# Two output bursts of eight key chunks per unit instead of three, and four fill products per step in the prologue

## The chip, the cores and the metric

The kernel runs on one core of a Trainium2 chip. The metric is the device time of one execution in microseconds (us), the median of several runs; less is better.

## What is computed

Two independent results stand side by side in the output, both in f32 with 2048 rows.

```python
# left half: attention, 32 query heads of width 32, one key head and one value head
q = (x @ wq).reshape(B, S, H, Dh).transpose(0, 2, 1, 3)
k, v = x @ wk, x @ wv
p = softmax(einsum("bhqd,bkd->bhqk", q, k) * Dh ** -0.5)
a = einsum("bhqk,bkd->bhqd", p, v).transpose(0, 2, 1, 3).reshape(B, S, H * Dh) @ wo
# right half: real part of a 2D DFT given as matrices
y = dft_seq_re @ (x2 @ dft_hid_re.T) - dft_seq_im @ (x2 @ dft_hid_im.T)
```

S is 2048 and D is 1024.

## The kernel before

Every engine's order is written out by hand: each instruction keeps its place in the program (the recording helper is line 79, so nearly all rows of the profile carry L79). TensorE (PE) has two kinds of work that are woven together.

**Fill products.** The query projections, the DFT and the output projection are groups of 12 or 24 matmuls of 128x512 into one PSUM bank (`psb`, two banks). An operand is split into a high and a low part, so that a product is three matmuls (`mh`/`ml` against `rh`/`rl`). `take(n)` issues the next n matmuls, `pos["fill"]` counts them, and `pump()` issues the loads, casts and subtractions that are due a given number of products ahead. Left operands live in a ring of NM slots: the cast of item i may only be issued once item i-NM has been used up. When a group is full, VectorE (DVE) takes it out of PSUM; for the query projections that is a TENSOR_SCALAR and a SCALAR_TENSOR_TENSOR (`q_group`).

**Attention.** A unit is four heads for 512 queries; there are 32 units with 32 steps each (SU), 1024 steps in all. A unit goes through two passes.

- The score pass (`scores`, `row_sums`) finds each query's log-sum. A step is two matmuls into a tile of `pss`, a pool of two PSUM tiles; DVE takes the maximum over it (TENSOR_REDUCE), ScalarE (ACT) then does exp in place and sums (ACTIVATE and its ACTIVATION_READ_ACCUMULATOR). After the last step of a unit `lse_1` to `lse_4` combine the sums with small operations, and one transpose (`nm` with `ident`), which also takes a `pss` tile, brings them into the layout that the next pass needs.
- The key pass (`expo`) makes the probabilities. A step is two matmuls into `pst`, one PSUM tile, and an exp on ACT into a tile of the pool `pp` (NP tiles named `p`). The output burst `pv(u, k)` then multiplies the tiles with `v`: four heads times the chunks between `CUT[k]` and `CUT[k + 1]`, as matmuls of 32 columns, which profile rows count twice (24 matmuls stand as x48). A chunk is two steps. DVE adds the burst's bank into `ov`.

The score pass runs LEAD steps and one whole unit ahead of the key pass. So the program has a prologue of SU + LEAD score steps with fill products between them and no key pass, then 1024 steps with a key pair each, in whose last SU + LEAD there are no scores left. `level(n)` spreads the remaining fill products over the steps; a step with a burst has none. `open_unit` loads a unit's queries (`qst`, three buffers), `inverse` loads the reciprocal sums (`rb`), and a unit's scaled output is made by GpSimd (POOL) in `ends` and stored to DRAM.

Of the kernel before, what the change touches and what calls it, by code (L numbers as in the profile page):

```python
# [8 lines left out]
F32 = mybir.dt.float32  # L9
F32R = mybir.dt.float32r  # L10
# [6 lines left out]
P = 128  # L17
# [4 lines left out]
W = 512  # L22
NG = 8
NQ = 4
NC = 16
# [76 lines left out]
def tile_kernel(ctx: ExitStack, tc, xT, wq, wkv, wo, xbT, wT, cT, out):  # L102
    nc = tc.nc
    te = Ordered(tc, nc.tensor)
    act = Ordered(tc, nc.scalar)
    dve = Ordered(tc, nc.vector)
    gp = Ordered(tc, nc.gpsimd)
# [3 lines left out]
    def pool(stack, name, bufs, **kw):  # L111
        kw.setdefault("reuse_waits", "tile")
        return stack.enter_context(tc.tile_pool(name=name, bufs=bufs, **kw))
# [17 lines left out]
    kst = keep.tile([P, S], F32R, name="kst")  # L131
# [6 lines left out]
    ps_t = pool(ctx, "ps_t", 1, space=PSUM)  # L138
    ps_b = [pool(ctx, f"ps_b{i}", 1, space=PSUM) for i in range(2)]

    NR0, NM0, NY = 3, 3, 6
    NR, NM = 14, 4
    r0p = pool(ctx, "r0p", NR0, side="right")
    m0p = pool(ctx, "m0p", NM0, side="right")
    rp = pool(ctx, "rp", NR)
# [43 lines left out]
    pos = {"fill": 0, "s": 0}  # L189
# [82 lines left out]
    ML = Line(NM0, NM, (52, 36, 27, 21), load_m, comb, hi_m, lo)  # L272
# [42 lines left out]
    def at(p, f):  # L315
        k = len(later)
        while k and later[k - 1][0] > p:
            k -= 1
        later.insert(k, (p, f))
# [33 lines left out]
    def bank(name, open_=False):  # L353

        while held:
            held.pop(0)()
        b = 1 - cur["bank"] if cur["bank"] is not None else int(used[1] < used[0])
        cur["at"] += 1
        used[b] = cur["at"]
        if open_:  # L360
            cur["bank"] = b
        return ps_b[b].tile([P, W], F32, name=name)
# [16 lines left out]
    def take(n):  # L379
        for _ in range(n):  # L380
            if cur["group"] >= len(groups):
                return
            g = groups[cur["group"]]
            j = pos["fill"] - g.at
            if j == 0:
                cur["ps"] = bank("psb", True)
            if j % 3 == 0:
                RL.force(g.right[j // 3])
            if j % 12 == 0:
                ML.force(g.left[j // 12])  # L390
            product(g, cur["ps"], j)
            pos["fill"] += 1
            if j == g.n - 1:
                cur["group"] += 1
                assert all(hasattr(it, "done") for it in g.ys)
                g.post(cur["ps"])
                cur["at"] += 1
                used[cur["bank"]] = cur["at"]
                cur["bank"] = None
                if g.ys:  # L400
                    at(pos["fill"] + 2 * BEHIND + 5, lambda n=len(g.ys): yused.__setitem__(0, yused[0] + n))
            pump()
            run_later()
# [300 lines left out]
    start = [q_group(0, g, sets[0]) for g in range(2)]  # L704
# [10 lines left out]

    qsp = pool(ctx, "qsp", 1)
    rows = []
    NP = 13
    pp = pool(ctx, "pp", NP, side="right")
    sm = pool(ctx, "sm", 2, side="right")  # L720
    onp = pool(ctx, "onp", 1, side="right")

    units = [(b, g) for b in range(NQ) for g in range(NG)]
    SU = 32
    LEAD = 12
    total = SU * len(units)
    qst, nm, lse, pt, ov, rb, pend = ({} for _ in range(7))
    ends = []
# [73 lines left out]
            r = r_d[u][4 * h:4 * h + 4].rearrange("t c -> (t c)")  # L802
            sp.dma_start(rb[u][h * DH:(h + 1) * DH], r.unsqueeze(0).to_broadcast([DH, W]))

    def expo(n):
        u, r = divmod(n, SU)
        c, hp_ = divmod(r, 2)
        pt[u, c, hp_] = pp.tile([P, 2, W], F32, name="p")
        ps = ps_t.tile([P, 2, W], F32, name="pst")
        for a in range(2):  # L810
            te.matmul(ps[:, a], kst[:, c * P:(c + 1) * P], qst[u][:, 2 * hp_ + a], start=True, stop=True)
        act.activation(pt[u, c, hp_], ps, AF.Exp)

    CUT = (0, 6, 11, NC)

    def blocks(d, g, x):
        return d[:, :, g].rearrange("t p c -> p t c"), x.rearrange("p (t c) -> p t c", t=4)

    def pv(u, k):

        aside()
        ps = bank("psb")
        for c in range(CUT[k], CUT[k + 1]):
            for h in range(4):
                te.matmul(ps[h * DH:(h + 1) * DH], v[:, c], pt[u, c, h // 2][:, h % 2], start=c == CUT[k], stop=c == CUT[k + 1] - 1)
        if k == 0:
            ov[u] = onp.tile([P, W], F32, name="ov")
            dve.tensor_copy(ov[u], ps)
        else:
            dve.tensor_add(ov[u], ov[u], ps)  # L830
        cur["at"] += 1
        if k == len(CUT) - 2:
            b, g = units[u]
            if b < 2:
                def scaled():
                    o = onp.tile([P, W], F32, name="oh")
                    gp.tensor_mul(o, ov[u], rb[u])
                    store(*blocks(o_d[b], g, o), ("o", b, g))
                ends.append(scaled)
                return  # L840
            hi_ = onp.tile([P, W], F32, name="oh").bitcast(F32R)
            lo_ = onp.tile([P, W], F32R, name="ol")
            lse["out"] = hi_, lo_

            last = u + 1 == len(units)
            e = dve if last else gp

            def low():
                e.tensor_sub(lo_, ov[u], hi_.bitcast(F32))
                if not last:  # L850
                    store(*blocks(oh_d[b], g, hi_))
                    store(*blocks(ol_d[b], g, lo_), ("o", b, g))

            ends.append(lambda: e.tensor_mul(ov[u], ov[u], rb[u]))
            ends.append(lambda: e.tensor_copy(hi_, ov[u]))
            ends.append(low)

    def score_step(s):

        if s < total:  # L860
            u, r = divmod(s, SU)
            if r == SU - 6 and u + 1 < len(units):
                open_unit(u + 1)
        if SU <= s < SU * (len(units) + 1) and s % SU == TURN:
            row_sums(s - 1)
            lse_3((s - SU) // SU)
        if s < total:
            scores(s)
        row_sums(s - 1)
        u, e = divmod(s - SU, SU)  # L870
        if 0 <= u < len(units):
            for f in LSE.get(e, ()):
                f(u)

    TURN = 3
    LSE = {0: (lse_1,), 1: (lse_1b,), 2: (lse_2,), 5: (lse_4,)}

    zeros = v[:, :, :].rearrange("p a b -> p (a b)")
    for n in (W, 3 * P):
        te.matmul(ps_t.tile([P, 2, W], F32, name="pst")[:, 0, :n], zeros[:, :P], zeros[:, :n], start=True, stop=True)  # L880
    room = [t[:, k] for t in [pp.tile([P, 2, W], F32, name="p") for _ in range(NP)] for k in range(2)]
    room += [r0p.tile([P, W], F32, name="r1", bufs=NR0 - 1) for _ in range(2)] + [onp.tile([P, W], F32, name="rb")]
    room += [m0p.tile([P, 4, P], F32, name="m1", bufs=NM0 - 1).rearrange("p a b -> p (a b)") for _ in range(2)]
    room += [r0p.tile([P, W], F32, name="r0", bufs=NR0)]
    xs = [[room[b * ND + c] for c in range(ND)] for b in range(NQ)]

    def load_x(b):
# [12 lines left out]
    wkv_t = onp.tile([P, W], F32, name="ov")  # L900
    sp.dma_start(wkv_t, wkv.rearrange("p a b -> p (a b)"))
    load_x(1)
    for it in start[1].left:
        ML.force(it)
    pump()
    load_x(2)
    load_x(3)
# [5 lines left out]
    take(48)  # L913
    for s in range(SU + LEAD):
        score_step(s)
        take(7)

    PRO = pos["fill"]
    FILL = end[0]
    LAST = 24  # L920


    QUIET = total - SU - LEAD
    MORE = 1

    def goal(n):
        return PRO + (FILL - PRO - LAST - MORE * (total - QUIET)) * n // total + MORE * max(n - QUIET, 0)


    ENDS = [2 * c for c in CUT]  # L930

    def snap(p):

        for d in (0, 1, -1, 2, -2, 3, -3):
            g = next((g for g in groups if g.at <= p + d < g.at + g.n), None)
            j = p + d - g.at if g else 0
            if j == 0 or 6 <= j <= g.n - 6:
                return p + d
        return p

    def level(n):
        r = n % SU
        if r in ENDS:
            return 0, 0
        more = min(e for e in ENDS if e > r) - r
        left = snap(goal(n + more)) - pos["fill"] - (2 if more > 2 else 0)
        fill = max(round(left / more), 0)
        return fill, min(fill, more, 2)

    for n in range(total):  # L950
        u, r = divmod(n, SU)
        if n == total - 12:
            w1 = wo_set(1)
            add([o_group(NQ - 1, t, e, ws) for e, ws in ((0, w0), (1, w1)) for t in range(4)])
        score_step(n + SU + LEAD)
        if ends:
            ends.pop(0)()
        fill, first = level(n)
        take(first)
        expo(n)  # L960
        if r == 16:
            inverse(u)
        if r in ENDS and n:
            pv((n - 1) // SU, (ENDS.index(r) - 1) % (len(CUT) - 1))
        take(fill - first)


    last = groups[len(groups) - 8:]
    take(last[0].at - pos["fill"] - 12)
    pv(len(units) - 1, len(CUT) - 2)  # L970
    while ends:
        ends.pop(0)()
    hi7, lo7 = lse["out"]
# [27 lines left out]
    for t, g in enumerate(last[4:]):  # L1001
        ps = whole(4 + t)
# [41 lines left out]
```

## Time and profile before

| what | value |
|---|---|
| median of 3 runs | 2695.97 us (2695.78 to 2699.55) |
| the profiled execution's own time | 2700.78 us |
| its span, first to last instruction | 2699.0 us |
| mean granted TensorE clock | 0.999 |
| matmul rows on PE | 13820 |

Durations below come from the one profiled execution. Its own time is 1.78 us more than its span and 4.81 us more than the median. A matmul's row is longer than its distance to the next row, since matmuls are pipelined: the distance between the starts is what a matmul costs.

### The profile page before, as it was taken

Reading aid. Unit: us, or ns where it says so; the run is one execution under the profiler, and the core shown is the slowest. Engines: PE = TensorE matmul, PEld = TensorE weight load, DVE = VectorE, ACT = ScalarE, POOL = GpSimd, SP = SyncE. Lnnn points to the kernel's source line nnn. Section 1 sums busy time; section 2 is a strip of 40 time slices with the busy share of each in tenths; the row PEclk is TensorE's granted clock in tenths of the full one; section 3 lists DMA queues with packets and bytes.
Section 4 is the critical chain, followed back from the end, with each engine's and each line's share of the span. In section 5 each row is a group of like instructions: output and inputs, shape, how many; then the busy total and the mean of one; then the engine's idle time right before and its main releaser. Section 6 shows DMA issues by size and latency. Waiting matters only on the chain. (4 is left out here: it accounts for less than half of the span.)

```text
span 2699.0 us, 40566 instructions
## 1 busy us (share of the span) xinstructions
PE 2689.4 (100%) x13820; PEld 1920.5 (71%) x13820; DVE 1593.1 (59%) x1826; ACT 2130.9 (79%) x3131; POOL 1723.3 (64%) x1711
## 2 busy tenths in 40 slices
PE   9999999999999999999999999999999999999999
PEld 6876767677676766767676676767677676766767
DVE  5766666666676665655565566666555555655411
ACT  3588888888888888888888888878888888888741
POOL 4854425776647558875556675576887887865741
PEclk9999999999999999999999999999999999999999
DMA  8543336887788666654445679874775765644665
GB/s 277 188 142 124 114 102 209 283 281 224 255 267 285 204 220 184 194 182 137 144 155 152 187 244 298 294 238 139 212 222 165 223 198 160 207 143 131 194 209 187
DMA packets 316931, 538.24 MB, mean 199 GB/s; under 512 B 35962, under 2 KB 63354, under 8 KB 316666
## 3 DMA queue, kind: packets, MB, share of 16 engines
q1 hardware_dynamic: 315572, 533.69, 62.5%
q8 instruction: 109, 1.79, 0.3%
q10 hardware_dynamic: 1152, 1.97, 0.2%
q14 instruction: 98, 0.80, 0.1%
HBM read 395.58 MB, written 138.15 MB: 198 GB/s over the span
## 5 line engine op out<-in xcount | busy, mean ns | idle before, releaser
L79 DVE TENSOR_REDUCE nm<-pss 128x1 f32<-128x1024 f32 x1024 | 1252.3, 1223 | 550.8 <-PE pss L79 549.7
L79 ACT ACTIVATE p<-pst 128x1024 f32<-128x1024 f32 x1026 | 1056.0, 1029 | 444.6 <-PE pst L79 435.0
L79 ACT ACTIVATE pss<-pss,nm 128x1024 f32<-128x1024 f32 x1024 | 1112.4, 1086 | 53.7 <-DVE nm L79 53.1
L79 PE MATMUL psb<-rh,mh 128*128 128x512 f32 x1790 | 699.2, 391 | 0.2 <-ACT rh L79 0.2
L79 PE MATMUL psb<-rl,mh 128*128 128x512 f32 x1790 | 698.4, 390 | 0.0
L79 PE MATMUL psb<-rh,ml 128*128 128x512 f32 x1790 | 698.3, 390 | 0.0
L79 PE MATMUL pss<-kst,qst 128*128 128x512 f32 x2048 | 642.8, 395 | 0.2
L79 PE MATMUL pst<-qst,kst 128*128 128x512 f32 x2048 | 635.8, 392 | 0.1
L79 POOL TENSOR_TENSOR ml<-m,mh 128x512 fp32r<-128x512 f32 x366 | 473.2, 1293 | 33.3 <-PE pss L79 26.3
L79 PEld LDWEIGHTS pss<-kst,qst 128*128 128x128 f32 x2048 | 375.6, 188 | 128.9 <-issue 51.1
L79 PE MATMUL psb<-p,v 128*32 128x512 f32 x4096 | 461.0, 596 | 3.1 <-DVE y L79 3.1
L79 PEld LDWEIGHTS pst<-qst,kst 128*128 128x128 f32 x2048 | 377.9, 188 | 92.2 <-ACT p L79 16.3
L79 PEld LDWEIGHTS psb<-rh,mh 128*128 128x128 f32 x1790 | 336.6, 188 | 75.9 <-issue 1.7
L79 PEld LDWEIGHTS psb<-rh,ml 128*128 128x128 f32 x1790 | 336.4, 188 | 72.8 <-issue 1.7
L79 PEld LDWEIGHTS psb<-rl,mh 128*128 128x128 f32 x1790 | 336.5, 188 | 71.8 <-DVE rl L79 0.5
L79 POOL CAST mh<-m 128x512 fp32r<-128x512 f32 x365 | 224.6, 615 | 234.1 <-PE psb L79 199.8
L79 PEld LDWEIGHTS psb<-p,v 128*32 128x32 f32 x4096 | 123.6, 110 | 287.6 <-issue 270.2
L79 POOL TENSOR_TENSOR m<-m,m 128x512 f32<-128x512 f32 x220 | 284.4, 1293 | 42.5 <-DMA m<-o 19.6
L79 POOL TENSOR_TENSOR rl<-r,rh 128x512 fp32r<-128x512 f32 x208 | 269.1, 1294 | 4.0
L79 POOL CAST rh<-r 128x512 fp32r<-128x512 f32 x208 | 128.5, 618 | 203.0 <-PE psb L79 152.2
L79 ACT ACTIVATION_READ_ACCUMULATOR pss<-pss,nm 128x1 f32 x1024 | 211.0, 206 | 0.0
L79 POOL TENSOR_TENSOR r<-r,r 128x512 f32<-128x512 f32 x120 | 155.2, 1293 | 62.0 <-DMA r<-in_wT_dram 44.7
(92 smaller groups left out, 791.9 us busy)
## 6 DMA issues: line engine op xcount, KB each, us to landing
m<-in_cT_dram SPq DMA_DIRECT2D x384, 256.0 KB
r<-s SPq DMA_DIRECT2D x192, 256.0 KB
y<-y SPq DMA_DIRECT2D x128, 256.0 KB
r<-in_wT_dram SPq DMA_DIRECT2D x88, 256.0 KB
m<-in_xbT_dram SPq DMA_DIRECT2D x88, 256.0 KB
y<-u SPq DMA_DIRECT2D x80, 256.0 KB
m<-in_wq_dram SPq DMA_DIRECT2D x64, 256.0 KB
qst<-qh SPq DMA_DIRECT2D x64, 256.0 KB
```

The lines of the kernel that those rows point to most:

```text
L79: return lambda *a, **k: self.tc.keep_in_program_order(f(*a, **k))
```

## The change

Each unit's output is multiplied out in two bursts of eight chunks instead of three of six, five and five. The burst follows the unit's step 15 or 31 directly and takes in the tile of that very step: the step's key matmuls come ahead of the burst and its exp is issued after the burst's first chunk, so 15 tiles of `p` (13 before) are enough. LEAD goes from 12 to 20 and the prologue's steps take four products instead of seven. The ring of left operands has three slots instead of four. A unit's scaled output is made in place in `ov` (and `rb`), not in tiles of its own. Queries are opened ten score steps ahead of their unit's first instead of six, the transpose comes one score step later (TURN), and the last burst of all lies inside the loop.

```diff
-    NR, NM = 14, 4
+    NR, NM = 14, 3
...
-    NP = 13
+    NP = 15
...
-    LEAD = 12
+    LEAD = 20
...
-    def expo(n):
+    def key_scores(n):
         u, r = divmod(n, SU)
         c, hp_ = divmod(r, 2)
-        pt[u, c, hp_] = pp.tile([P, 2, W], F32, name="p")
         ps = ps_t.tile([P, 2, W], F32, name="pst")
         for a in range(2):
             te.matmul(ps[:, a], kst[:, c * P:(c + 1) * P], qst[u][:, 2 * hp_ + a], start=True, stop=True)
+        return ps
+
+    def key_exp(n, ps):
+        u, r = divmod(n, SU)
+        c, hp_ = divmod(r, 2)
+        pt[u, c, hp_] = pp.tile([P, 2, W], F32, name="p")
         act.activation(pt[u, c, hp_], ps, AF.Exp)
 
-    CUT = (0, 6, 11, NC)
+    CUT = (0, NC // 2, NC)
+    LASTS = [2 * c - 1 for c in CUT[1:]]
...
-    def pv(u, k):
+    def pv(u, k, between):
...
                 te.matmul(ps[h * DH:(h + 1) * DH], v[:, c], pt[u, c, h // 2][:, h % 2], start=c == CUT[k], stop=c == CUT[k + 1] - 1)
+            if c == CUT[k]:
+                between()
...
-                    o = onp.tile([P, W], F32, name="oh")
-                    gp.tensor_mul(o, ov[u], rb[u])
+                    gp.tensor_mul(o, o, r)
...
-            if r == SU - 6 and u + 1 < len(units):
+            if r == SU - 10 and u + 1 < len(units):
                 open_unit(u + 1)
...
-    TURN = 3
+    TURN = 4
...
     for s in range(SU + LEAD):
         score_step(s)
-        take(7)
+        take(4)
 
     PRO = pos["fill"]
     FILL = end[0]
-    LAST = 24
+    LAST = 12
...
-        expo(n)
+        ps = key_scores(n)
         if r == 16:
             inverse(u)
-        if r in ENDS and n:
-            pv((n - 1) // SU, (ENDS.index(r) - 1) % (len(CUT) - 1))
+        if r in LASTS:
+            pv(u, LASTS.index(r), lambda: key_exp(n, ps))
+        else:
+            key_exp(n, ps)
         take(fill - first)
...
-    take(last[0].at - pos["fill"] - 12)
-    pv(len(units) - 1, len(CUT) - 2)
     while ends:
         ends.pop(0)()
```

The program's order on PE shows the two places. First, the start of the prologue: a score step is the pair into `pss` and the products (`psb`) behind it. Before:

```order
L79 MATMUL pss<-kst,qst_758 128x512 x2
L79 MATMUL psb<-rh,mh 128x512
L79 MATMUL psb<-rl,mh 128x512
L79 MATMUL psb<-rh,ml 128x512
L79 MATMUL psb<-rh,mh 128x512
L79 MATMUL psb<-rl,mh 128x512
L79 MATMUL psb<-rh,ml 128x512
L79 MATMUL psb<-rh,mh 128x512
L79 MATMUL pss<-kst,qst_758 128x512 x2
```

After the change, on the same engine at the same place:

```order
L79 MATMUL pss<-kst,qst_756 128x512 x2
L79 MATMUL psb<-rh,mh 128x512
L79 MATMUL psb<-rl,mh 128x512
L79 MATMUL psb<-rh,ml 128x512
L79 MATMUL psb<-rh,mh 128x512
L79 MATMUL pss<-kst,qst_756 128x512 x2
```

Between two score pairs three products are gone; there are 52 such steps (of 208 products) instead of 44 (of 308). Second, PE around a burst (`psb<-p,v`) in mid-attention, the last one of a unit. Before:

```order
L79 MATMUL pss<-kst,qst_2057 128x512 x2
L79 MATMUL pst<-qst_1386,kst 128x512 x2
L79 MATMUL psb<-p,v 32x512 x20
L79 MATMUL pss<-kst,qst_2057 128x512 x2
L79 MATMUL psb<-rh,mh 128x512
```

The same with the change:

```order
L79 MATMUL pss<-kst,qst_1632 128x512 x2
L79 MATMUL pst<-qst_756,kst 128x512 x2
L79 MATMUL psb<-p,v 32x512 x32
L79 MATMUL pss<-kst,qst_1632 128x512 x2
L79 MATMUL psb<-rh,mh 128x512
```

The neighbours of a burst are the same and the burst is longer; over the program there are 64 of 32 matmuls where there were 32 of 24 and 64 of 20. Steps between bursts keep the pattern of pair, two products, pair, three products nearly everywhere.

## Rows read from the trace of the kernel before

**Rows 1.** The page: busy us of each engine, share of the span, instructions.

```profile
PE 2689.4 (100%) x13820; PEld 1920.5 (71%) x13820; DVE 1593.1 (59%) x1826; ACT 2130.9 (79%) x3131; POOL 1723.3 (64%) x1711
```

**Rows 2.** Windows, mid-attention: stretch, length, busy (x count) by engine, clock, DMA.

```profile
300.00:1000.00 700.00, 700.00 (x3640) 498.52 (x3642) 456.65 (x533) 589.24 (x868) 405.52 (x397) 1.00 0.70 228
```

**Rows 3.** The list of waits: total us, times, longest.

```profile
POOL mh L79 <- PE psb L79: 199.8, 80, 9.5
...
PEld pst L79 <- ACT p L79: 16.3, 79, 0.5
...
PE psb L79 <- DVE y L79: 3.1, 1, 3.1
```

**Rows 4.** Timeline of PE around two bursts, of six and of five chunks.

```profile
1026.00 5.36 PE L79 MATMUL psb<-p,v 128*32 128x512 f32 x48
1031.28 0.74 PE L79 MATMUL pss<-kst,qst 128*128 128x512 f32 x2
...
1075.36 0.61 PE L79 MATMUL pst<-qst,kst 128*128 128x512 f32 x2
1075.90 4.50 PE L79 MATMUL psb<-p,v 128*32 128x512 f32 x40
1080.33 0.73 PE L79 MATMUL pss<-kst,qst 128*128 128x512 f32 x2
1080.90 0.39 PE L79 MATMUL psb<-rh,ml 128*128 128x512 f32 x1
```

**Rows 5.** Timeline of PE in the prologue: two score pairs that follow each other.

```profile
65.64 0.61 PE L79 MATMUL pss<-kst,qst 128*128 128x512 f32 x2
...
67.68 0.61 PE L79 MATMUL pss<-kst,qst 128*128 128x512 f32 x2
```

**Rows 6.** Timeline: one `pss` tile, from its score pair to its next one.

```profile
134.32 0.61 PE L79 MATMUL pss<-kst,qst 128*128 128x512 f32 x2
...
134.97 1.23 DVE L79 TENSOR_REDUCE nm<-pss 128x1 f32<-128x1024 f32 x1 [0.40 <-PE pss L79]
...
136.29 1.09 ACT L79 ACTIVATE pss<-pss,nm 128x1024 f32<-128x1024 f32 x1 [0.42 <-DVE nm L79]
...
137.30 0.19 ACT L79 ACTIVATION_READ_ACCUMULATOR pss<-pss,nm 128x1 f32 x1
...
137.55 0.72 PE L79 MATMUL pss<-kst,qst 128*128 128x512 f32 x2
```

**Rows 7.** Timeline of PE in the prologue: score pairs around the first transpose.

```profile
114.62 0.61 PE L79 MATMUL pss<-kst,qst 128*128 128x512 f32 x2
...
117.85 0.72 PE L79 MATMUL pss<-kst,qst 128*128 128x512 f32 x2
```

**Rows 8.** Timeline in the prologue: DVE between two maxima, with a score pair.

```profile
102.11 0.68 DVE L79 TENSOR_SCALAR qh<-psb 128x512 fp32r<-128x512 f32 x1
...
102.36 0.61 PE L79 MATMUL pss<-kst,qst 128*128 128x512 f32 x2
...
102.83 0.69 DVE L79 SCALAR_TENSOR_TENSOR y<-psb,qh 128x512 fp32r<-128x512 f32 x1
...
103.44 1.22 DVE L79 TENSOR_REDUCE nm<-pss 128x1 f32<-128x1024 f32 x1
```

**Rows 9.** Timeline of PE near the end: key pairs, no scores left.

```profile
2606.96 0.70 PE L79 MATMUL pst<-qst,kst 128*128 128x512 f32 x2
...
2608.86 0.70 PE L79 MATMUL pst<-qst,kst 128*128 128x512 f32 x2
```

**Rows 10.** Timeline (DVE, PE) at PE's long idle time; windows there and at the transpose.

```profile
1759.78 0.69 DVE L79 TENSOR_TENSOR y<-y,psb 128x512 f32<-128x512 f32 x1 [3.48 <-DMA y<-c]
...
1760.53 6.20 PE L79 MATMUL psb<-p,v 128*32 128x512 f32 x40 [3.14 <-DVE y L79]
...
1762.00:1763.50 1.50, 1.50 (x12) 0.43 (x8) 0.46 (x3) 0.91 (x2) 0.24 (x1) 0.50 1.01 320
...
116.00:118.20 2.20, 1.44 (x7) 0.77 (x6) 2.10 (x9) 1.21 (x2) 1.41 (x2) 1.00 0.01 4
```

More of the change, by code (lines that the diff above doesn't have):

```diff
@@ L803, in inverse @@
             sp.dma_start(rb[u][h * DH:(h + 1) * DH], r.unsqueeze(0).to_broadcast([DH, W]))
-    def expo(n):
+    def key_scores(n):
+        u, r = divmod(n, SU)
+        c, hp_ = divmod(r, 2)
+        ps = ps_t.tile([P, 2, W], F32, name="pst")
+        for a in range(2):
+            te.matmul(ps[:, a], kst[:, c * P:(c + 1) * P], qst[u][:, 2 * hp_ + a], start=True, stop=True)
+        return ps
+    def key_exp(n, ps):
         u, r = divmod(n, SU)
@@ L808, in expo @@
         pt[u, c, hp_] = pp.tile([P, 2, W], F32, name="p")
-        ps = ps_t.tile([P, 2, W], F32, name="pst")
-        for a in range(2):
-            te.matmul(ps[:, a], kst[:, c * P:(c + 1) * P], qst[u][:, 2 * hp_ + a], start=True, stop=True)
         act.activation(pt[u, c, hp_], ps, AF.Exp)
-    CUT = (0, 6, 11, NC)
+    CUT = (0, NC // 2, NC)
+    LASTS = [2 * c - 1 for c in CUT[1:]]
     def blocks(d, g, x):
         return d[:, :, g].rearrange("t p c -> p t c"), x.rearrange("p (t c) -> p t c", t=4)
-    def pv(u, k):
+    def pv(u, k, between):
         aside()
@@ L833, in pv @@
             b, g = units[u]
+            o, r = ov[u], rb[u]
             if b < 2:
                 def scaled():
-                    o = onp.tile([P, W], F32, name="oh")
-                    gp.tensor_mul(o, ov[u], rb[u])
+                    gp.tensor_mul(o, o, r)
                     store(*blocks(o_d[b], g, o), ("o", b, g))
@@ L840, in pv @@
                 return
-            hi_ = onp.tile([P, W], F32, name="oh").bitcast(F32R)
-            lo_ = onp.tile([P, W], F32R, name="ol")
-            lse["out"] = hi_, lo_
+            hi_, lo_ = r.bitcast(F32R), o.bitcast(F32R)
             last = u + 1 == len(units)
             e = dve if last else gp
+            if last:
+                both = pp.tile([P, 2, W], F32, name="p").bitcast(F32R)
+                hi_, lo_ = both[:, 0], both[:, 1]
+                lse["out"] = hi_, lo_
             def low():
-                e.tensor_sub(lo_, ov[u], hi_.bitcast(F32))
+                e.tensor_sub(lo_, o, hi_.bitcast(F32))
                 if not last:
@@ L852, in low @@
                     store(*blocks(ol_d[b], g, lo_), ("o", b, g))
-            ends.append(lambda: e.tensor_mul(ov[u], ov[u], rb[u]))
-            ends.append(lambda: e.tensor_copy(hi_, ov[u]))
+            ends.append(lambda: e.tensor_mul(o, o, r))
+            ends.append(lambda: e.tensor_copy(hi_, o))
             ends.append(low)
@@ L881, in tile_kernel @@
     room = [t[:, k] for t in [pp.tile([P, 2, W], F32, name="p") for _ in range(NP)] for k in range(2)]
-    room += [r0p.tile([P, W], F32, name="r1", bufs=NR0 - 1) for _ in range(2)] + [onp.tile([P, W], F32, name="rb")]
-    room += [m0p.tile([P, 4, P], F32, name="m1", bufs=NM0 - 1).rearrange("p a b -> p (a b)") for _ in range(2)]
-    room += [r0p.tile([P, W], F32, name="r0", bufs=NR0)]
+    room += [r0p.tile([P, W], F32, name="r1", bufs=NR0 - 1) for _ in range(2)]
     xs = [[room[b * ND + c] for c in range(ND)] for b in range(NQ)]
@@ L902, in tile_kernel @@
     load_x(1)
-    for it in start[1].left:
-        ML.force(it)
+    ML.force(start[1].left[0])
     pump()
@@ L927, in goal @@
         return PRO + (FILL - PRO - LAST - MORE * (total - QUIET)) * n // total + MORE * max(n - QUIET, 0)
-    ENDS = [2 * c for c in CUT]
     def snap(p):
@@ L942, in level @@
         r = n % SU
-        if r in ENDS:
+        if r in LASTS:
             return 0, 0
-        more = min(e for e in ENDS if e > r) - r
-        left = snap(goal(n + more)) - pos["fill"] - (2 if more > 2 else 0)
+        more = min(e for e in LASTS if e > r) - r
+        left = snap(goal(n + more + 1)) - pos["fill"] - (2 if more > 2 else 0)
         fill = max(round(left / more), 0)
@@ L959, in tile_kernel @@
         take(first)
-        expo(n)
+        ps = key_scores(n)
         if r == 16:
             inverse(u)
-        if r in ENDS and n:
-            pv((n - 1) // SU, (ENDS.index(r) - 1) % (len(CUT) - 1))
+        if r in LASTS:
+            pv(u, LASTS.index(r), lambda: key_exp(n, ps))
+        else:
+            key_exp(n, ps)
         take(fill - first)
     last = groups[len(groups) - 8:]
-    take(last[0].at - pos["fill"] - 12)
-    pv(len(units) - 1, len(CUT) - 2)
     while ends:
```

## The prediction

> **What bounds the kernel now.** I read the page first: PE is the one engine that is busy all through, at a mean granted clock of 0.999; ACT follows with 79% [rows 1]. A busy matrix engine need not be a limited one, so I went on to windows of single stretches: in mid-attention PE has no idle time in 700 us [rows 2]. Then the list of waits, for those of PE and its weight loads: 16.3 us in 79 small pieces behind ACT's exps and one wait of 3.1 us behind DVE are the largest that name another engine, and none is on POOL [rows 3]. So the time is the number of matmuls times their distance, plus a few stalls. The distance of ordinary matmuls is read from a prologue step: two score matmuls and seven products, 2.04 us from pair to pair [rows 5], 0.227 us each. The change leaves the number of matmuls of every kind as it is. It can only change two things: what a matmul costs at the edges of bursts, and where PE has to wait.
>
> **Removed: 32 burst edges.** Around a burst of five chunks, key pair to burst is 0.54 us where a pair normally takes 0.45 (twice 0.227), burst to score pair is 4.43, and the score pair takes 0.57 until the next product: 0.09 and 0.12 too much. A burst of six chunks takes 5.28 to its score pair, so a chunk is 0.85 (0.86 by the bursts' own lengths) and 4.43 holds 0.13 to 0.18 that belongs to no chunk [rows 4]. An edge pair so costs 0.34 to 0.39 us; I take 0.36. Three bursts become two in each of 32 units: 32 x 0.36 = 11.5 us gained (10.9 to 12.5). The Trainium skill speaks of this too: TensorEngine Tiling (Array Packing), section Key Properties, says that a change of tiling mode drains TensorE, and TensorE: Matmul & The Clock Gate, section Single matmul latency, has 398 cycles at 2.4 GHz of latency beside the columns, 0.17 us. Two such drains for each burst would be 0.33 us, an estimate from these pages, and the gain 10.6 us instead of 11.5.
>
> **Moved: 100 products, out of the prologue.** This is where I expect the loss. A prologue step will have two score matmuls and four products, 6 x 0.227 = 1.36 us of PE. But a `pss` tile goes round through three engines before PE may write it again. The rows follow one: score pair at 134.32, maximum at 134.97, exp at 136.29, its sums from 137.30 for 0.19, and the next pair in that tile at 137.55, 0.06 after they end [rows 6]. That is 3.23 us, and with two tiles no step can be shorter than 1.615 us on average. The prologue's steps of before (2.04) feel it at two places alone: at its end, where [rows 6] stand, and where the transpose takes a tile and two pairs are 3.23 us apart [rows 7], the same round. With steps of 1.36 the round is the limit in all of the prologue. Its costs:
>
> - 50 of 52 steps (the first two find both tiles free) lose 1.615 - 1.36 = 0.255: 12.7 us.
> - The transpose takes one turn of the two tiles, so one step waits a whole round: 1.6 us more. Before, that place lost 3.23 - 2.04 = 1.2 us [rows 7].
> - DVE also empties a query group every 24 products, now every six steps, with two operations of 0.7 us. In the rows the maximum starts 1.08 us after its score pair instead of 0.65, 0.43 late [rows 6, 8]. With slack in the round that cost nothing; now it lengthens the round. At 1.615 a step DVE has some 0.5 us free beside its maximum, so I put it at 0.36 for each of 208 / 24 = 8.7 groups: 3.1 us (0 if it hides, 6 if both operations count in full).
> - The small operations on the log-sum of the first unit, some 0.6 us, likewise.
>
> Together 18.0 us, less the 1.2 of before: 16.8 us lost, from 11.5 (only the round) to 20. The products that move into the attention cost there what they cost anywhere, since PE is full; they fill nothing that stands idle.
>
> **The tail.** With no scores left, a step of six products and a key pair should take 8 x 0.227 = 1.81 us and takes 1.90 [rows 9], because the one `pst` tile goes round through ACT. The stretch without scores grows from 44 to 52 steps; by the order, 39 instead of 33 of them have six products. 6 x 0.09 = 0.5 us lost.
>
> **At nothing.** The longer burst: the exp of its last tile waits for the first chunk (0.85 us) and is needed by the eighth, 6 us into the burst, while ACT has one row sum left; if it were late, PE would wait in all 64 bursts. The ring of three: POOL already waits for PE there, 80 times [rows 3]. Each such cast can now start 12 products later, but still 24 products ahead of its first use, which at five products in 2.04 us is 9.8 us; PE has no wait on POOL now. If this cover fails in places where POOL is crowded, 0 to 5 us. Scaling in `ov` and `rb`: the next write into `ov` comes 16 steps, over 30 us, after the burst, and the store starts two to four steps after it. The earlier opening of queries puts their loads ahead in SP's queue, with some 20 us until their first use instead of 12; their buffer is free three steps before. The step structure between bursts is the same, so ACT and DVE keep pace as before.
>
> **The base.** The profiled execution took 2700.78 us, 4.8 above the median. It contains one long idle time: a load of `y` came late, DVE waited 3.48 us, the burst behind it 3.14; then the clock fell (0.50 in a window of that burst) and the burst took 6.20 instead of 4.50 us [rows 4, 10]. 3.1 + 1.7 = 4.8 us: I take it that the median's executions do not have it. 2700.8 - 4.8 - 11.5 + 16.8 + 0.5 = 2701.8 us, which is the median of 2695.97 plus 5.8. A measurement of this kernel can tell about 0.2%, 5.4 us, from no change; the forecast stands just above that.
>
> **Rivals.**
>
> - *Faster: the round does not bind.* The prologue would have to run at PE's 1.36 us a step. Then only the edges count: 2696.0 - 11.5 - 1.2 + 0.5 = 2683.8. It needs a round of at most 2.72 us. Against it: 3.23 twice, at two places [rows 6, 7], and the parts of a round are durations of single instructions that no order shortens.
> - *Same: only the round.* DVE's other work and the transpose fit into the round's slack: 2696.0 - 11.5 + 11.5 + 0.5 = 2696.5. For it: DVE is idle for 0.40 us before the maximum in [rows 6].
> - *Same: the long stall was in the median and goes.* 2701.8 - 4.8 = 2697.0. The runs of before spread over 3.8 us, which looks like a stall that comes and goes; their two lowest lie together.
> - *Slower by more: such a stall comes in.* Loads, stores and group ends shift against each other in SP's queue and against the longer bursts, and the stall of [rows 10] is of that kind: 2701.8 + 4.8 = 2706.6.
> - *Much slower: the clock falls in the prologue.* PE would be idle for 0.25 us or more in each step. In [rows 10] it fell after an idle time of 3.14 us, and stayed at 1.00 in the window of the transpose's wait. At the lower level of 1.2 GHz a step would be 6 x 0.453 = 2.72 us, 1.1 us over the round: 52 x 1.1 = 57, 2759. The Trainium skill, TensorE: Matmul & The Clock Gate, in its table on why this matters for kernels, warns of idle gaps between bursts of matmuls; the row of the 3.14 us agrees, and no row has many short gaps.
>
> **How the numbers follow.** Chances: the forecast 0.50 (its own range 2698 to 2706, of which some six parts in ten lie above the bound of 2701.4); only the round 0.15; the stall goes 0.09; a stall comes in 0.15; the clock 0.03; faster 0.08. Slower is 0.30 + 0.15 + 0.03 = 0.48, same 0.20 + 0.15 + 0.09 = 0.44, faster 0.08. The range reaches from the cases of the same time down to where only the faster one is left out, 2695, and up to a stall on top of the forecast with the upper bound of DVE's share, 2708.
>
> **What would show it.** In the profile after: score pairs in the prologue 1.6 us apart on average and not 1.36, with PE idle before them and released by ACT's sums; the time from the first score pair to the first key pair near 89 us, where PE alone needs 70.7; around bursts the same 0.36 us, with 64 bursts, and 6.9 us from burst to score pair; key pairs near the end still 1.90 apart; no wait of PE on POOL. The prediction is wrong if score pairs come at 1.36 us, if PE waits inside the bursts or behind casts of left operands, or if the edges of the longer bursts cost more than those of before.

## The result, and the profile after

The changed kernel takes 2709.24 us (median of 6 runs, 2705.72 to 2710.11) against 2696.59 of the kernel before on the same chip (6 runs, 2695.78 to 2699.55). The ratio is 1.0041 [1.0031, 1.0051]: slower by 8.4 to 13.8 us, where 5.8 were forecast. The median lies 1.2 us above the range's upper end of 2708.0; by the ratio the loss is 11.1 us, which put on the 2695.97 of the prediction would lie inside it. The profiled execution took 2709.79 us, with a span of 2708.0.

Busy time says little here either. The page's line of after, to be laid beside [rows 1]:

```profile
PE 2693.2 (99%) x13820; PEld 1924.8 (71%) x13820; DVE 1567.4 (58%) x1794; ACT 2126.9 (79%) x3130; POOL 1734.1 (64%) x1712
```

PE has as many rows as before and is busy for 3.8 us more, in a span that is 9.0 us longer. The waits tell more. The list of waits of after (total us, times, longest), beside [rows 3]:

```profile
POOL mh L79 <- PE psb L79: 298.4, 115, 11.3
POOL ov L79 <- DVE ov L79: 242.3, 30, 19.8
PEld pss L79 <- ACT pss L79: 30.4, 60, 2.4
PEld pst L79 <- ACT p L79: 15.4, 69, 0.6
DVE y L79 <- DMA y<-c: 7.7, 4, 2.7
PE pss L79 <- ACT pss L79: 4.0, 5, 2.0
PE psb L79 <- DVE y L79: 1.8, 1, 1.8
```

PE and its weight loads now wait for ACT to give back a `pss` tile (30.4 and 4.0 us; 4.8 before). Most of that is the prologue (24.6 us up to the first key pair). DVE waits four times for a load of `y` from `c`, where it waited once. There is still no wait of PE on POOL.

**The prologue.** The timeline of PE and of the engines that a `pss` tile goes through, first at the start, then one round in the middle, then the step with the transpose:

```profile
46.10 0.62 PE L79 MATMUL pss<-kst,qst 128*128 128x512 f32 x2
47.46 0.62 PE L79 MATMUL pss<-kst,qst 128*128 128x512 f32 x2
49.41 0.74 PE L79 MATMUL pss<-kst,qst 128*128 128x512 f32 x2 [0.43 <-ACT pss L79]
...
88.26 0.73 PE L79 MATMUL pss<-kst,qst 128*128 128x512 f32 x2
88.83 0.39 PE L79 MATMUL psb<-rl,mh 128*128 128x512 f32 x1
88.55 0.68 DVE L79 SCALAR_TENSOR_TENSOR y<-psb,qh 128x512 fp32r<-128x512 f32 x1
89.15 1.21 DVE L79 TENSOR_REDUCE nm<-pss 128x1 f32<-128x1024 f32 x1
90.46 1.09 ACT L79 ACTIVATE pss<-pss,nm 128x1024 f32<-128x1024 f32 x1 [0.52 <-DVE nm L79]
91.47 0.19 ACT L79 ACTIVATION_READ_ACCUMULATOR pss<-pss,nm 128x1 f32 x1
91.71 0.73 PE L79 MATMUL pss<-kst,qst 128*128 128x512 f32 x2
...
105.21 0.74 PE L79 MATMUL pss<-kst,qst 128*128 128x512 f32 x2
108.26 0.73 PE L79 MATMUL pss<-kst,qst 128*128 128x512 f32 x2 [1.15 <-DVE mt L79]
...
135.24 0.73 PE L79 MATMUL pss<-kst,qst 128*128 128x512 f32 x2
```

The first two steps are 1.36 us apart, PE's own pace; the third pair already waits. In the round, the group's second DVE operation holds the maximum back until 89.15, and the next pair starts 0.05 us after ACT's sums end (91.66): 3.45 us, of which 3.23 were known from [rows 6]. From the first pair (46.10) to the 53rd (135.24) are 89.1 us, 1.71 a step.

**The bursts.** PE's timeline around the second burst of a unit, to be laid beside [rows 4]:

```profile
1075.38 0.61 PE L79 MATMUL pst<-qst,kst 128*128 128x512 f32 x2
1075.92 7.07 PE L79 MATMUL psb<-p,v 128*32 128x512 f32 x64
1082.92 0.73 PE L79 MATMUL pss<-kst,qst 128*128 128x512 f32 x2
```

Key pair to burst 0.54, burst to score pair 7.00 for eight chunks: the edges are those of before, and there are 64 in place of 96.

**Late loads.** Two units in mid-run are long. The first key pairs of unit 20 and of unit 21 stand at 1713.23 and 1796.20, and that of unit 22 at 1879.20: 83.0 us each, where unit 4, with as many matmuls (284 and 16 chunks), takes 78.9 (451.61 to 530.49). The timeline of unit 21's case, in order of cause (SP's queue, POOL, DVE, ACT, PE):

```profile
1794.32 0.30 SPq L79 DMA_DIRECT2D qst<-qh  x1
1801.70 0.83 SPq L79 DMA_DIRECT2D m<-in_cT_dram  x2
1809.83 1.77 SPq L79 DMA_DIRECT2D y<-c  x2
...
1784.20 1.28 POOL L79 TENSOR_TENSOR rl<-r,rh 128x512 fp32r<-128x512 f32 x1
1796.09 1.29 POOL L79 TENSOR_TENSOR ov<-ov,rb 128x512 f32<-128x512 f32 x1 [10.61 <-DVE ov L79]
1800.38 1.30 POOL L79 TENSOR_TENSOR ml<-m,mh 128x512 fp32r<-128x512 f32 x1
...
1816.29 1.35 DVE L79 TENSOR_TENSOR y<-y,psb 128x512 f32<-128x512 f32 x2 [2.66 <-DMA y<-c]
1817.56 2.35 DVE L79 TENSOR_REDUCE nm<-pss 128x1 f32<-128x1024 f32 x2
1818.87 1.09 ACT L79 ACTIVATE pss<-pss,nm 128x1024 f32<-128x1024 f32 x1 [2.35 <-DVE nm L79]
1820.12 0.97 PE L79 MATMUL pss<-kst,qst 128*128 128x512 f32 x2 [2.02 <-ACT pss L79]
```

Windows ahead of PE's wait and behind it (columns as in [rows 2]):

```profile
1815.50:1817.50 2.00, 2.00 (x11) 1.60 (x10) 1.21 (x2) 1.02 (x2) 1.92 (x3) 1.00 1.00 352
1820.50:1823.50 3.00, 3.00 (x9) 2.33 (x8) 1.22 (x1) 2.24 (x4) 3.00 (x3) 0.50 0.84 267
```

Read from the top. POOL ends a subtraction at 1785.5 and then stands for 10.61 us in front of the scaling of `ov`, which needs the end of the unit's burst. Its casts and subtractions are queued behind that. SP has nothing issued from 1794.62 to 1801.70, the moment at which POOL's next `ml` is done. The loads of `y` follow late, at 1809.83; DVE waits 2.66 us for them at 1816.29, with two maxima behind it; ACT waits for the maxima, and PE for ACT. Behind the wait the clock is at 0.50, 1.2 GHz, where it was at 1.00. The DMA engines are full here (share 1.00 in the first window), and DVE's wait ends 6.5 us after the first of the two loads was issued. The Trainium skill, Perfetto Trace Analysis, section Tensor Engine Instruction (MATMUL, LD_WEIGHTS), says that ACT, DVE and GPSIMD take their instructions in strict order; the rows agree, and all of this chain hangs on it.

Unit 20's wait comes earlier and is of the kind of [rows 10], which stands in the same unit: DVE waits 2.15 us for a load of `y` (1785.20) and the burst 1.79 us for DVE (1786.69), the clock falls there too, and POOL's wait of 10.61 us ends only at 1796.09. What stands ahead of it in the trace is a wait of POOL for a load of a right operand (`r<-s`, 4.64 us, at 1769.24) and one of SP's queue for POOL's subtraction behind that (4.5 us). Units 8 and 9 have smaller waits of DVE, 1.0 and 2.1 us, for loads of `y` from another tensor, `u`.

**The account.** For every stretch I subtract from its length what its PE rows cost at 0.227 us for an ordinary matmul and 0.858 for a chunk; what remains is edges, waits and clock. All from PE's rows of the two profiled executions:

| stretch | before | after | difference |
|---|---|---|---|
| until the first score pair | 45.21 | 46.10 | +0.9 |
| prologue, first score pair to first key pair (399 and 317 matmuls) | 1.2 | 18.3 | +17.2 |
| edges, 31 units: each unit's remainder where it is least, 1.13 and 0.73 | 35.0 | 22.6 | -12.4 |
| units 7 to 9, 20 and 21, beyond that | 6.3 | 10.9 | +4.6 |
| the other 26 units, beyond that | 4.8 | 3.9 | -1.0 |
| last unit | 3.9 | 3.7 | -0.3 |
| sum; spans 2699.0 and 2708.0 | | | +9.0 |

Of the 6.3 us of before, 5.5 belong to the one stall of [rows 10], which the median's executions don't have. Of the 10.9 of after, unit 7's 0.8 is no late load: the unit has 278 matmuls and not 284, no load makes it wait, and the first experiment shows what such a number costs. So against the median the late loads of units 8, 9, 20 and 21 cost some 9 us, and they are the largest part of what the forecast lacked.

### The profile page after: what moved, and what is told of

Read it like the earlier page. It is cut to its first block, busy times and chain, and to the rows that moved or that the text cites. A ratio compares the mean times of both kernels' runs of the same rounds, so it can differ in the third digit from the quotient of the medians.

```text
span 2708.0 us, 40395 instructions
## 1 busy us (share of the span) xinstructions
PE 2693.2 (99%) x13820; PEld 1924.8 (71%) x13820; DVE 1567.4 (58%) x1794; ACT 2126.9 (79%) x3130; POOL 1734.1 (64%) x1712
## 3 DMA queue, kind: packets, MB, share of 16 engines
q8 instruction: 109, 1.79, 0.3%
## 4 chain that ended last, share of the span: by engine, by line
PE 94%; DVE 2%; DMA 1%; ACT 1%; issue 1%; POOL 0%; SPq 0%; DVEq 0%; ACTq 0%; POOLq 0%
PE psb L79 59%; PE pss L79 18%; PE pst L79 17%; DVE nm L79 1%; ACT pss L79 1%; DMA y<-c 0%; DMA y<-u 0%; DVE y L79 0%; SPq L79 0%; POOL ml L79 0%; DMA p<-in_xT_dram 0%; DVE qh L79 0%; DMA r<-s 0%; POOL rl L79 0%; DMA r<-in_xT_dram 0%
## 5 line engine op out<-in xcount | busy, mean ns | idle before, releaser
L79 PE MATMUL psb<-p,v 128*32 128x512 f32 x4096 | 454.2, 595 | 1.8 <-DVE y L79 1.8
L79 PEld LDWEIGHTS pst<-qst,kst 128*128 128x128 f32 x2048 | 378.9, 188 | 91.5 <-ACT p L79 15.4
L79 POOL CAST mh<-m 128x512 fp32r<-128x512 f32 x366 | 224.6, 614 | 332.5 <-PE psb L79 298.4
L79 POOL TENSOR_TENSOR ov<-ov,rb 128x512 f32<-128x512 f32 (+1 forms) x46 | 59.4, 1291 | 247.5 <-DVE ov L79 242.3
```

Of the source, the lines that this page charges most:

```text
L79: return lambda *a, **k: self.tc.keep_in_program_order(f(*a, **k))
```

## The experiments

Each was measured beside the kernel before, whose median was 2696.97 us beside the first four below (six and four products, third tile, ring of three), 2697.11 beside those with `y` earlier, the ring of four with the change and five products, 2696.74 beside the three with POOL's scaling later in the changed kernel or the third tile and the ring of four, and 2696.86 beside the last. The interval of each ratio reaches 2 to 4 us to either side.

**Six products in the prologue** (changed kernel):

```diff
-        take(4)
+        take(6)
```

> The change with six products per prologue step instead of four. Theory of the round: a step then has eight matmuls, 8 x 0.227 = 1.81 us, more than half a round of a pss tile (3.36 to 3.45 us measured between pairs two steps apart in the changed kernel), so PE waits at the transpose alone; of the 18.3 us of excess in the prologue some 1.5 to 2.5 stay, and the time falls by 15 to 17 us, to 2690 to 2694, below the kernel before (2696.6). Rival, that the loss lies in the attention (late loads of y, the ring of three, longer bursts): the time stays within 3 us of the changed kernel's 2709.

Measured: 2696.76 us, 0.9999 [0.999, 1.0008], above the expected 2690 to 2694. The prologue's remainder fell from 18.3 to 1.25 us, but the time by 12.5 only. The attention gave part of it back, 8.5 us in the trace's 26 other units: with 104 products fewer, many steps have four, 8 x 0.227 = 1.81 us of PE. The list of waits of this kernel, where the changed kernel has 15.4 us in 69:

```profile
PEld pst L79 <- ACT p L79: 27.8, 136, 0.6
```

The timeline of ACT, then of PE, in such steps:

```profile
509.32 1.04 ACT L79 ACTIVATE p<-pst 128x1024 f32<-128x1024 f32 x1
510.23 1.11 ACT L79 ACTIVATE pss<-pss,nm 128x1024 f32<-128x1024 f32 x1
...
511.31 1.06 ACT L79 ACTIVATE p<-pst 128x1024 f32<-128x1024 f32 x1
...
508.59 0.62 PE L79 MATMUL pst<-qst,kst 128*128 128x512 f32 x2
510.53 0.63 PE L79 MATMUL pst<-qst,kst 128*128 128x512 f32 x2
```

ACT has no gap (the sums of the score step, 511.22 to 511.45, overlap the next exp) and needs 1.99 us for a step's exps (509.32 to 511.31), so PE's key pairs of a step of four products are 1.94 apart. Unit 4 has six matmuls fewer than in the changed kernel (278), 1.36 us, and is only 0.69 shorter (78.18). Products in the prologue are not free even where the round doesn't bind: the attention needs them to be bound by PE.

**Four products in the prologue of the kernel before**, with its three bursts:

```diff
-        take(7)
+        take(4)
```

> The kernel before with four products per prologue step and nothing else changed (LEAD 12, three bursts, ring of four). Theory of the round: 44 score steps at 1.72 us where PE needs 1.36, so about 42 x 0.36 = 15 us of waiting, plus 1.4 at the transpose, less the 1.2 that the kernel before lost there: 2696.6 + 15 = 2710 to 2713. Rival, that the prologue is free of waits and the loss comes from the rest of the change: no change, 2695 to 2699.

Measured: 2710.11 us, 1.005 [1.0037, 1.0062]. Four products in the prologue alone make the kernel before slower by as much as the whole change. The prologue's remainder is 16.0 us there. In the attention 28 of 31 units have a remainder of 1.12 to 1.17, which in the kernel before only 13 have: the products that moved did fill idle time, 4.1 us over the units without a stall.

A late load comes in here as well: unit 21 has a remainder of 4.9. Its timeline (POOL, DVE):

```profile
1788.20 1.29 POOL L79 TENSOR_TENSOR ov<-ov,rb 128x512 f32<-128x512 f32 x1 [6.65 <-DVE ov L79]
...
1808.70 0.69 DVE L79 TENSOR_TENSOR y<-y,psb 128x512 f32<-128x512 f32 x1 [3.43 <-DMA y<-c]
```

Between the two, SP's queue waits 7.6 us for a subtraction of POOL, until 1793.70. It is the chain of the changed kernel, with bursts of five and six chunks and a ring of four. So the products that moved are enough to bring a late load in; neither the longer burst nor the smaller ring is needed. That POOL's wait is its cause in this kernel is read from the rows and was not tested here.

**A third tile in the prologue** (changed kernel): every third score step takes the `pst` tile, which is idle there.

```diff
+        if s < SU + LEAD and s % 3 == 2:
+            ps = ps_t.tile([P, 2, W], F32, name="pst").rearrange("p a w -> p (a w)")
+        else:
+            ps = ps_s.tile([P, 2 * W], F32, name="pss")
-        ps = ps_s.tile([P, 2 * W], F32, name="pss")
```

> The change, but in the prologue every third score step uses the PSUM tile of the key pass, which has no work there: three tiles go round instead of two. Theory of the round: a step may then be as short as 3.36 / 3 = 1.12 us, PE's 1.36 is the limit again or DVE's (1.14 for a maximum and 1.3 per six steps for a query group, 1.36 to 1.40), so 13 to 17 of the 18.3 us of waiting go: 2692 to 2696. If DVE alone were the limit and not the number of tiles: no gain, 2706 to 2710.

Measured: 2693.53 us, 0.9984 [0.9975, 0.9993]: faster than the kernel before. PE's timeline in its prologue:

```profile
70.98 0.62 PE L79 MATMUL pss<-kst,qst 128*128 128x512 f32 x2
72.34 0.62 PE L79 MATMUL pss<-kst,qst 128*128 128x512 f32 x2
73.70 0.62 PE L79 MATMUL pst<-kst,qst 128*128 128x512 f32 x2
```

1.36 us, PE's pace, with the same products and the same clock: what bound the prologue was the number of tiles. 15.7 us came back. Units 20 and 21 (2.9 and 5.1 us of remainder) and unit 9 (2.1) are long in its trace; the late loads stayed. Two expectations below give 7.3 us for unit 21 and 2.8 for unit 9, or speak of units 9 and 21 alone: they count the 17 prologue pairs in `pst` as key pairs, so that their units begin half a unit too early.

**A ring of three in the kernel before** (and only the first left operand ahead):

```diff
-    NR, NM = 14, 4
+    NR, NM = 14, 3
```

> The kernel before with three slots for left operands instead of four (and the second left operand of the second group not forced ahead, as in the change). Theory that the ring of three delays loads: POOL's casts wait later for PE, SP's loads behind them come later, loads of y among them, and DVE and PE wait for those: 2 to 6 us slower, 2699 to 2703, with more idle time of PE between 800 and 1850 us. Rival, that the ring has slack: within 1.5 us of the kernel before.

Measured: 2698.66 us, 1.0006 [0.9997, 1.0015]. No difference that the runs can tell; the median lies 1.7 us higher, and up to 4 us are inside the interval. The smaller ring alone is not the loss.

**Loads of `y` earlier** (changed kernel):

```diff
-        while ydone[0] < min(len(ylist), yused[0] + NY) and ylist[ydone[0]].due - 24 <= pos["fill"]:
+        while ydone[0] < min(len(ylist), yused[0] + NY) and ylist[ydone[0]].due - 36 <= pos["fill"]:
```

> The changed kernel with one number altered: a load of y is put into SP's queue 36 products ahead of its use instead of 24, some 5 us earlier; PE's order is the same. Theory (late loads: DVE waits for y because its load is issued late behind other entries of SP's queue, and about 11 us of PE's idle time and low clock in units 7 to 9, 20 and 21 hang on it): those units fall to 0.7 to 1.4 us of excess, 2699 to 2704. Rival (the transfers themselves are short of bandwidth there, so an earlier place only delays the others): DVE waits for y as before or POOL and DVE for r and s instead, 2707 to 2711.

Measured: 2714.75 us, 1.0067 [1.0054, 1.008]. Both theories missed: it is 5.5 us slower. What SP's queue waits for between 1700 and 1840 us, in the changed kernel:

```profile
SPq L79 <- DMA c<-y: 2.5, 6, 0.8
```

The same here:

```profile
SPq L79 <- DMA c<-y: 23.3, 10, 4.8
```

And the timeline here at PE's longest wait in the attention (DVE, PE):

```profile
1737.94 0.69 DVE L79 COPY qh<-psb 128x512 f32<-128x512 f32 x1 [5.22 <-DMA c<-qh]
...
1741.71 1.22 PE L79 MATMUL pss<-kst,qst 128*128 128x512 f32 x2 [4.58 <-ACT pss L79]
```

The load reads from `c` what a store wrote there shortly before. Placed earlier, it waits at the head of SP's queue for that store to land, and everything behind it waits too. The longest such wait, 4.8 us, ends when a load of `y` is issued at 1729.19. A store of `qh` stands behind it and is issued at 1732.90; DVE waits for that store 5.22 us, and PE 4.58 us by the maxima and exps that come after. Later loads of `y` are late as well (DVE's longest wait for one is 5.42 us, at 1788.67, instead of 2.66), and here PE does wait for POOL, 2.62 us at 1789.46 for the cast of a left operand. Unit 20 has 12.4 us of remainder.

**The ring of four with the change** (13 right operands instead of 14 make room):

```diff
-    NR, NM = 14, 3
+    NR, NM = 13, 4
```

> The changed kernel with four slots for left operands again (and 13 instead of 14 for right operands, to make room); bursts of eight and four products in the prologue stay. Theory (the ring of three blocks POOL, whose late low parts hold up the entries behind them in SP's queue): SP's waits for POOL shrink, the late loads with them, 2699 to 2704. Rival (the ring has nothing to do with it; the queue is full because all loads of this phase are): 2707 to 2711, or a little slower by the smaller ring of right operands.

Measured: 2705.93 us, 1.0032 [1.002, 1.0045]. It lies 3.3 us under the changed kernel, with overlapping intervals, and misses the expected 2704 by 2. The remainders of units 20 and 21 are 2.0 and 3.3 us instead of 4.8 and 4.9. The ring has at most a part in the late loads.

**Third tile and `y` earlier** (both edits above):

> The third prologue tile (2693.5 measured with it) and y loaded 36 products ahead together. If the late loads cost what the windows of its trace show (some 10 us in units 9 and 21) and the earlier place in the queue mends them, 2684 to 2689, faster than before by 0.3 to 0.5%. If the transfers are short of bandwidth, 2691 to 2695 as without it.

Measured: 2700.74 us, 1.0015 [1.0006, 1.0024], 7.2 us more than with the third tile alone. The same reading as above: units 20 and 21 have 10.9 and 5.0 us of remainder instead of 2.9 and 5.1, and PE waits 3.09 us for POOL at 1770.69.

**Five products in the prologue** (changed kernel):

```diff
-        take(4)
+        take(5)
```

> The changed kernel with five products per prologue step. PE's step is 7 x 0.227 = 1.59 us against a measured 1.72 on average: the prologue's loss falls from 18.3 to about 7 us. The attention has 5.08 products a step instead of 5.13. Theory (two opposed terms: the round of two tiles in the prologue, and ACT's pace of steps of four products in the attention, which appears little by little as products leave it): 2697 to 2702. Rival (only the round counts): 2695 to 2698.

Measured: 2705.9 us, 1.0037 [1.0024, 1.0051], above both expectations. The prologue's remainder is 11.5 us and not 7; DVE's group posts and the transpose are likely to lengthen the round still, but their shares were not separated. Units alternate between 0.73 and 1.5, as expected of ACT's pace, and units 20 and 21 have 3.4 and 7.6. In three points (four, five, six products) the prologue loses 18.3, 11.5 and 1.3 us, and the attention takes part of it back.

**POOL's scaling later** (changed kernel): the deferred work on a unit's output, POOL's scaling and the stores behind it, starts six steps into the next unit.

```diff
-        if ends:
+        if ends and r >= 6:
             ends.pop(0)()
```

> The changed kernel in which POOL's scaling of a unit's output is issued six steps later, so that POOL, which takes its work in order, no longer stands still until the burst has ended (242.3 us in 30 waits for ov, one of 10.6 us right ahead of the late loads at 1800 to 1820 us). PE's order is the same. Theory (POOL stands still, its casts and subtractions come late, SP's queue waits for those and the loads of y behind it come late too): POOL's wait for ov falls below 60 us, units 20 and 21 fall from 4.8 to 1 to 3 us of excess, 2701 to 2705. Rival (POOL has caught up by the time that y is loaded, the loads are late for another reason): 2707 to 2711.

Measured: 2702.87 us, 1.0021 [1.0012, 1.003], 6.4 us less than the changed kernel. POOL's wait for `ov` fell from 242.3 to 5.9 us, but it doesn't stand still much less: its wait for slots of left operands, 298.4 us in the changed kernel, stands in this list of waits as:

```profile
POOL mh L79 <- PE psb L79: 417.9, 138, 11.3
```

The timeline of SP, POOL and DVE at the place of the late loads:

```profile
1796.99 0.83 SPq L79 DMA_DIRECT2D m<-in_cT_dram  x2
1804.08 1.38 SPq L79 DMA_DIRECT2D y<-c  x2
...
1794.90 0.61 POOL L79 CAST mh<-m 128x512 fp32r<-128x512 f32 x1 [6.88 <-PE psb L79]
...
1810.75 1.28 DVE L79 TENSOR_TENSOR y<-y,psb 128x512 f32<-128x512 f32 x2
```

The load that came late is issued 5.75 us earlier (1804.08 for 1809.83), while the unit itself starts 2.7 earlier, and DVE no longer waits for it. Unit 21 is back at 0.75 us, unit 9 at 0.73. Unit 20 still has 3.8: the mechanism is a large part of the late loads, not all, and the wait for `r<-s` ahead of unit 20 is the same here (4.66 us at 1767.46). POOL still stands for 6.88 us here, now for a slot of the ring of three, which opens when PE goes on with products after the burst. The DMA engines are as full as they were (share 0.94 from 1780 to 1800 us and 0.95 from 1800 to 1820; 0.94 and 0.85 in the changed kernel), so full transfers alone do not make unit 21 long. Of the 5.75 us, 4.71 are there at the load of `m`, which follows POOL (1796.99 for 1801.70). The rest is that two stores of the unit's output, which stood ahead of the loads of `y` (1805.12 to 1806.35), now stand behind them. What each of the two is worth was not tested apart.

**Third tile and POOL's scaling later** (both edits above):

> The third prologue tile and the later scaling together. If the loads of y come in time with it, unit 21 falls from 7.3 and unit 9 from 2.8 us to 1 or 2: 2685 to 2690, 0.3 to 0.45% faster than before. If POOL's wait has nothing to do with it, 2691 to 2695 as with the third tile alone.

Measured: 2686.26 us, 0.996 [0.9948, 0.9973], within what was expected. This is the fastest version: 10.5 us under the kernel before and 23.0 under the changed kernel. Units 9 and 21 are at 0.7 and 0.8 us instead of 2.1 and 5.1, just as with two tiles; unit 20 is not better (4.6 instead of 2.9).

**Third tile and the ring of four** (both edits above):

> The third prologue tile with four slots for left and 13 for right operands. With two tiles that ring gave 3.3 us (2705.9 against 2709.2). If that is the ring's own worth, 2689 to 2691 here. If it only moved the late loads against each other by chance, anywhere in 2690 to 2696.

Measured: 2690.34 us, 0.9976 [0.9966, 0.9985], 3.2 us under the third tile alone, again with overlapping intervals. Twice 3 us speak for a small worth of the ring of its own, but units 8, 9, 20 and 21 have 2.7, 2.7, 1.6 and 4.9 us here, no less in sum than the 1.3, 2.1, 2.9 and 5.1 there. Where the 3 us come from stays open.

**POOL's scaling later in the kernel before** (the same edit as above):

> The kernel before with the same later issue of POOL's scaling (in its trace POOL waits 207.8 us in 29 pieces for ov). It tells whether POOL's wait is part of what the change costs. Theory (the change made it worse: the longer burst keeps POOL waiting longer): the kernel before gains 0 to 2 us, 2695 to 2697, and with the later scaling in both kernels the change costs 6 to 8 us, what the prologue and the edges alone make. Rival (the wait hurt before just as much): 2689 to 2692, and the change still costs 11 us.

Measured: 2696.01 us, 0.9995 [0.9986, 1.0004]. Nothing that the runs can tell, although the wait goes here as well, from 207.8 us in 29 pieces to what this row of the list of waits holds:

```profile
POOL oh L79 <- DVE ov L79: 8.0, 1, 8.0
```

With the later scaling in both kernels the change costs 2702.87 - 2696.01 = 6.9 us; without it, 12.7 by the medians. So some 6 us of the loss come from the meeting of POOL's work on the output, in its early place, with the changed order. The other 7 are not the forecast's terms alone: between the traces of the two versions with later scaling, units 8 and 20 still make up nearly 4 us by late loads.

## Why the prediction was right or wrong

- **Direction: right. The reason given for it: right, but not the whole of it.** The terms that the prediction summed to 5.8 us came to 17.2 - 12.4 - 0.3 = 4.5, less than the 5.4 us that it took a measurement to be able to tell. That the kernel is slower beyond doubt is owed to the late loads, which stood at nothing; in so far the direction was luck. The round of two `pss` tiles was forecast at 16.8 us and is 17.2. A third tile removes it, and the same prologue in the kernel before adds 14.8 us of remainder there (16.0 for 1.2). Its parts were less exact than their sum: a round is 3.45 us in the rows above and not 3.23, partly by DVE's posts and partly since a pair that has waited takes 0.57 us until the next row (88.26 to 88.83) and not 0.45; the transpose's step is 3.05 us (105.21 to 108.26), where 3.2 were forecast. How much of the 17.2 is DVE's share was not separated.
- **Removed: 32 burst edges.** Forecast 11.5, measured 0.40 for each instead of 0.36: 12.8. Above the own range of 10.9 to 12.5 by a little. The estimate from the Trainium skill's drains (TensorEngine Tiling (Array Packing), section Key Properties; TensorE: Matmul & The Clock Gate, section Single matmul latency) was 10.6, too low by more; the row was the better guide.
- **The tail.** Forecast +0.5; measured -0.3 for the whole last unit with its one edge of 0.40, so about +0.1. Key pairs near the end are still 1.91 apart, beside [rows 9].
- **At nothing: "fill nothing that stands idle" was wrong.** Steps of four products are bound by ACT, and the kernel before has them in most units; [rows 3] had shown it, 16.3 us of PE's weight loads behind ACT's exps, and I had not asked what moves them. Worth 4.1 us with three bursts (second experiment), 1.0 in the changed kernel.
- **At nothing: loads, stores and POOL.** This is the step that failed. The text looked for waits of PE on POOL, found none then and there are none now, and took the cover to hold. But the chain goes POOL, SP's queue, the load of `y`, DVE, the maxima, ACT, PE, and shows as a wait of PE for ACT. The rival of a stall that comes in had the right mechanism and half the price: 4.8 us for one, where the trace after has about 10 in four units. Nor was it a chance event: the profiled execution is within 0.6 us of the median, and a later scaling takes 6 us away. The chance of 0.15 was too low. The rows were there: the list of waits of before holds POOL's 207.8 us behind DVE's `ov`, which the prediction passed over as idle time of an engine that PE doesn't wait for:

```profile
POOL oh L79 <- DVE ov L79: 114.8, 14, 17.8
POOL ov L79 <- DVE ov L79: 93.0, 15, 11.1
```

- **The base.** That the 4.8 us of [rows 10] are not in the median holds in the main: 27 further runs of the kernel before have a median of 2696.97 us, 3.8 under the profiled execution, and reach 2700.3. The base of 2696.0 was about 1 us too low.
- **The rivals.** *Faster: the round does not bind* was refuted for this kernel, and its sum of 2683.8 is nearly what the version with the third tile and the later scaling reaches (2686.3). *The clock falls in the prologue* did not come: many short waits left it at its upper level. In the attention it fell around single idle times of 1.79 and 2.02 us.

What stays open: why POOL's wait costs nothing in the kernel before, where 8.50 us ahead of 1791.53 are followed by no late load, and 6.65 us do cost with four products in the prologue; what makes unit 20 long after all; and the worth of the ring of four. The version with the third tile, the later scaling and the ring of four was not run.

## What to carry to other kernels

Before work is taken out of a loop to shorten it, follow one buffer around: the number of buffers times the pace wanted must exceed the round, and here a PSUM tile that stood idle in the prologue turned a loss of 0.4% into a gain. An engine with idle time that takes its work in order can still be the cause of a stall: ask what is queued behind the instruction that waits, and which loads wait for that. A load may also come too early: if it reads what a store has just written, it blocks its queue until the store has landed.

## What the runs showed of the hardware

- The clock fell to 0.50 around two idle times of PE in the changed kernel, 1.79 us (until 1786.69) and 2.02 us (until 1820.12), both shorter than the 3.14 of [rows 10]. It stayed at 1.00 after single idle times of 2.21 us with six products (until 784.32) and 2.26 us with the later scaling (until 1785.50), so the length of one idle time does not settle it. It stayed at 1.00 in the prologue too, where PE's weight loads wait nearly 0.5 us in almost every step (23.8 us in 50 times). The Trainium skill, TensorE: Matmul & The Clock Gate, section HAM oscillation — how this bites in real kernels, warns of idle gaps between matmuls; for some of the single ones the traces agree, for others not, and the short ones of the prologue did nothing. A window of the prologue, columns as in [rows 2]:

```profile
48.00:104.00 56.00, 54.13 (x199) 34.51 (x198) 46.44 (x48) 39.92 (x68) 34.17 (x37) 1.00 0.44 139
```

- A pair of matmuls that had to wait takes 0.57 us until the next row instead of 0.45 (88.26 in the changed kernel), like the first pair after a burst. A wait costs more than its idle time, 0.12 us here.
